# A fused attention and bilinear feed-forward kernel: the first batch's chain by token halves, the first up weights in 256 columns, the down weight in six transfers

## Chip, cores and metric

The kernel runs on one core of a Trainium2 chip (trn2). The metric is the device time of one execution in microseconds (us). The kernel before has a median of 243.78 us over five runs, from 243.56 to 244.42 us.

## What is computed

Eight batches of eight attention heads (576 tokens, head size 64) are reduced through 32 memory slots, and the result goes through a bilinear feed-forward layer. Cut to what matters:

```python
a   = softmax(phi, axis=2)                       # 8 x 8 x 576 x 32
k_m = einsum('bhsm,bhsd->bhmd', a, k)            # 32 keys per head
v_m = einsum('bhsm,bhsd->bhmd', a, v)            # 32 values per head
x   = softmax(q @ k_m.T / 8) @ v_m               # 4608 tokens x 512
out = ((x @ w_a) * (x @ w_b)) @ w_out            # 512 -> 1536 -> 512
```

Inputs and output are float32 in DRAM; inside, the kernel works in float16.

## The kernel before, in words

**Stages of one batch.** `exp_phi` (`exp0`, `exp1`) takes the exponentials of `phi` on ScalarE. `sums` (`ks0`, `ks1` for keys, `vs0`, `vs1` for values; 0 and 1 are the two groups of four heads) is 36 small products on TensorE that give the unnormalised means and their denominators. VectorE then takes a reciprocal (L265) and scales the mean (`kvm`, L266). `transpose` (`kt0`, `kt1`, `vt0`, `vt1`) turns the mean on TensorE, and VectorE copies the result out of PSUM into `kvT` (L277). `q_transpose` (`qt0` to `qt3`, L204) turns q on VectorE. `scores` (`s0`, `s1`) needs `kvT` and two of the four turned q pieces; `exp_scores` (`e0`, `e1`) is ScalarE. `denominators` (`den0`, `den1`) is a product with a matrix of ones for each half of the 576 tokens, followed by a logarithm on ScalarE (L316); `normalise` (`nr0`, `nr1`) is an exponential on ScalarE (L324) and a product on VectorE (L326) that gives the attention weights `A`.

**Fold and up.** The output of attention is never formed. `fold` (`v0a`: columns 0 to 511 of w_a; `v1b`: columns 512 to 1023 of w_b; the names with h, such as `hv0a`, take 256 columns) multiplies the means of the values into the up weights, and `take_fold` (`x0a` and so on) copies the two PSUM banks out as `vab`, one on ScalarE and one on VectorE. `up_half` then multiplies `vab` with `A` for 128 of the 1536 columns and one half of the tokens (288): `a3` is column block 3 of the w_a side for both halves, `a3.0` its first half, `b3` the w_b side. ScalarE copies the a side out (L601), VectorE multiplies it with the b side into `ht` (L604). One 256-column load therefore serves blocks 0 and 1, a 512-column load blocks 0 to 3.

**Down.** The first four blocks of 128 tokens are multiplied with `w_out` directly (`early_downs`, L390): 4 blocks by 12 products of 512 columns. They are handed out one product at a time wherever a plan says `y3` (three products). The order runs over parts of `w_out`: every block gets its products with part 0 before any gets part 1. All later blocks go in pairs through seven sums instead of eight (`two_downs`, L465), planned by a class `Work` that spreads products over the slots of a stage.

**What sets the order.** The schedule is written by hand. `chain(0, ...)` and `chain(1, ...)` are strings of the unit names above in the order of issue; each engine runs its own instructions in this order. `f8` in a string is eight products of zeros (`fill`, L151), which nothing reads. From batch 1 on, `ups` runs the up blocks and hangs other units on the slots between them. PSUM has eight banks, which `Banks` hands out in turn.

**Loads.** The first batch's k comes by two transfers on the queues of SyncE and ScalarE. All other loads are issued by GpSimd (POOL) in one queue, converting float32 to float16 on the way (phi stays float32). Their order before is: phi, q (two halves), v of batch 0; w_a and w_b columns 0 to 511; 512 to 1023; 1024 to 1535; the first third of w_out; phi, k and the first half of q of batch 1; the second third of w_out; the second half of q; v in two halves; the last third of w_out; and then batch 2 and batch 3. A load on this queue waits for the load eight places before it: the page of waits shows GpSimd's `phi` load waiting for `v` of batch 0, and each later one for the load eight places ahead. After them GpSimd computes `w_sums` (L432), sums of parts of w_out.

Of the kernel before, what the change touches and what calls it, by code (L numbers as in the profile page):

```python
# [8 lines left out]
F32 = mybir.dt.float32  # L9
F16 = mybir.dt.float16  # L10
AF = mybir.ActivationFunctionType
ALU = mybir.AluOpType

P = 128
CS = 16.0
# [3 lines left out]
def kernel(  # L19
# [11 lines left out]
    nc = tc.nc  # L31
# [44 lines left out]
    def load_phi(b):  # L76
        phis[b] = inp.tile([P, NHP, NI * M], F32, name="phi_sb")
        nc.gpsimd.dma_start(out=phis[b], in_=rows(phi, b))

    def load_k(b, hps=slice(0, NHP)):  # L80
        kvs[b] = kv_sbs[b % 2]
        nc.gpsimd.dma_start(out=kvs[b][:, 0, hps], in_=rows(k, b)[:, hps])

    def load_v(b, hps=slice(0, NHP)):
        nc.gpsimd.dma_start(out=kvs[b][:, 1, hps], in_=rows(v, b)[:, hps])

    def load_q(b, hps=slice(0, NHP)):
        if b not in qs:
            qs[b] = inp.tile([P, NHP, NI * D], F16, name="q_sb")
        nc.gpsimd.dma_start(out=qs[b][:, hps], in_=rows(q, b)[:, hps])  # L90
# [7 lines left out]
    def load_wab(lo, hi):  # L98
        nc.gpsimd.dma_start(out=wa_sb[:, :, lo:hi], in_=wa_rows[:, :, lo:hi])
        nc.gpsimd.dma_start(out=wb_sb[:, :, lo:hi], in_=wb_rows[:, :, lo:hi])  # L100

    def load_wo(n):
        sl = slice(4 * n, 4 * (n + 1))
        nc.gpsimd.dma_start(out=wo_sb[:, sl, :], in_=wo_rows[:, sl, :])


# [48 lines left out]
    nc.vector.memset(kv_sbs[0][:, 2], 1.0 / CS)  # L155
    for x in halves:
        nc.vector.tensor_copy(out=kvs[0][:, 0, x], in_=k_f32[:, x])
    load_wab(0, 512)

    ones = consts.tile([P, 4, 32], F16, name="ones")  # L160
    nc.vector.memset(ones, 1.0)
# [2 lines left out]
    nc.gpsimd.affine_select(out=ones, in_=ones, compare_op=ALU.is_ge, fill=0.0, base=31,  # L164
                            pattern=[[32, 4], [0, 32]], channel_multiplier=-1)
    load_wab(512, 1024)
    load_wab(1024, 1536)
    load_wo(0)
    load_phi(1)
    load_k(1)  # L170
    load_q(1, halves[0])
    load_wo(1)
    load_q(1, halves[1])
    for x in halves:
        load_v(1, x)
    load_wo(2)
    nc.gpsimd.memset(kv_sbs[1][:, 2], 1.0 / CS)

    attn = {}
    vabs = {}  # L180
# [6 lines left out]
    def units(b):  # L187
# [57 lines left out]
        def sums(g, x):  # L245

            if g == 0 and x == 0:
                t["kvm"] = mid.tile([P, 2, 2, D], F16, name="kvm")
                t["rphi"] = small.tile([P, 2], F32, name="rphi")
                t["kvT"] = mid.tile([P, 6, P], F16, name="kvT")  # L250
            part = (slice(0, 3, 2), slice(1, 2))[x]
            pk = banks.tile([P, 2 - x, D], F32, name="pk")
            for i in range(NI):
                for j in range(4):
                    r, hp = head(g, j)
                    nc.tensor.matmul(  # L256
                        pk[32 * j:32 * j + 32],
                        t["exp"][64 * r:64 * r + 64, hp, i, :],
                        kvs[b][64 * r:64 * r + 64, part, hp, D * i:D * (i + 1)],
                        start=(i == 0),  # L260
                        stop=(i == NI - 1),
                        tile_position=(64 * r, 32 * j),
                    )
            if x == 0:
                nc.vector.reciprocal(out=t["rphi"][:, g:g + 1], in_=pk[:, 1, 0:1])  # L265
            nc.vector.tensor_scalar(out=t["kvm"][:, g, x], in0=pk[:, 0], scalar1=t["rphi"][:, g:g + 1], scalar2=None,  # L266
                                    op0=ALU.mult)

        def transpose(g, x):
            pT = banks.tile([P, 2 - x, P], F16, name="pT")  # L270
            for y in range(2 - x):
                for z in range(4):
                    cols = (slice(y, D, 2), slice(32 * (z % 2), 32 * (z % 2) + 32))[x]
                    nc.tensor.transpose(out=pT[32 * z:32 * z + 32, y, :], in_=t["kvm"][:, g, x, cols],
                                        identity=ident, tile_position=(0, 32 * z))
            lo = 4 + g if x else 2 * g
            nc.vector.tensor_copy(out=t["kvT"][:, lo:lo + 2 - x], in_=pT)  # L277

        def scores(gs):
            if 0 in gs:  # L280
# [25 lines left out]
                nc.scalar.activation(out=Ev[:, g, :, z, :], in_=pss, func=AF.Exp, scale=1.0 / (8.0 * CS))  # L306
                banks.free(bank)

        def denominators(g):

            t["L", g] = small.tile([P, S], F32, name="L")
            for hf in range(2):
                sl = slice(HALF * hf, HALF * (hf + 1))
                pD = banks.tile([P, HALF], F32, name="pD")
                nc.tensor.matmul(pD, ones, t["E"][:, g, sl], start=True, stop=True)  # L315
                nc.scalar.activation(out=t["L", g][:, sl], in_=pD, func=AF.Ln)  # L316
# [36 lines left out]
        def one(f, *a):  # L353
            return lambda: f(*a)

        for z in range(2):
            u[f"exp{z}"] = one(exp_phi, z)
            u[f"ks{z}"] = one(sums, z, 0)
            u[f"kt{z}"] = one(transpose, z, 0)
            u[f"vs{z}"] = one(sums, z, 1)  # L360
            u[f"vt{z}"] = one(transpose, z, 1)
            u[f"s{z}"] = one(scores, (z,))
            u[f"e{z}"] = one(exp_scores, z)
            u[f"den{z}"] = one(denominators, z)
            u[f"nr{z}"] = one(normalise, z)
            for hf in range(2):
                u[f"nr{z}{hf}"] = one(normalise, z, slice(hf, hf + 1))
            for n in range(NCH):
                u[f"v{n}{'ab'[z]}"] = one(fold, 512 * n, 512 * (n + 1), (z,))
                u[f"x{n}{'ab'[z]}"] = one(take_fold, 512 * n, 512 * (n + 1), z)  # L370
            for n in range(2):
                u[f"hv{n}{'ab'[z]}"] = one(fold, 256 * n, 256 * (n + 1), (z,))
                u[f"hx{n}{'ab'[z]}"] = one(take_fold, 256 * n, 256 * (n + 1), z)
# [13 lines left out]
    def down_part(po, bank, cidx, lo, hi):  # L387
        pair, c = divmod(cidx, NI)
        for i in range(lo, hi):
            nc.tensor.matmul(po, ht[:, i, P * c:P * (c + 1)], wo_sb[:, i, :],  # L390
                             start=(i == 0), stop=(i == NFF - 1))
            if i == NFF - 1:
                banks.free(bank)
                o_sb = opool.tile([P, d_model], F32, name="o_sb")
                nc.scalar.mul(out=o_sb, in_=po, mul=1.0 / (CS * CS))
                for z in range(2):
                    slot = 2 * c + z
                    nc.sync.dma_start(out=out_rows[2 * pair + slot // NI, slot % NI],
                                      in_=o_sb[64 * z:64 * z + 64, :])
            yield  # L400
# [8 lines left out]
    def early_downs():  # L409

        pos = [banks.take([P, d_model], F32, "po", hold=True) for c in range(EARLY)]
        for n in range(3):
            for c in range(EARLY):
                yield from down_part(*pos[c], c, 4 * n, 4 * (n + 1))

# [248 lines left out]
    def chain(b, plan):  # L666


        for x in plan.split():
            if x[0] == "f":  # L670
                fill(int(x[1:]), 256)
            elif x[0] == "y":
                some(int(x[1:]))
            elif x[0] in "ab":
                i, _, hf = x[1:].partition(".")
                for h in ([int(hf)] if hf else (0, 1)):
                    up_half(b, int(i), h, "ab".index(x[0]))
            else:
                us[b][x]()

    fill(16)
    chain(0, "exp0 exp1 qt0 qt1 f12 ks0 f4 kt0 f2 ks1 f1 s0 e0 kt1 qt2 qt3 f2 den0 f4 s1 e1 nr0 f8 vs0 vs1 den1 f2 vt0 vt1 nr1 f4")
    chain(0, "v0a x0a f4 a0 a1 v0b x0b f4 b0 b1 a2 b2 v1a x1a a3 b3 a4 a5 v1b x1b a6 a7 b4 b5 v2a x2a b6 b7 a8 a9")
    load(2)
    chain(0, "v2b x2b a10 a11 b8 b9 b10 b11")
    chain(1, "exp0 y1 exp1 y11 ks0 ks1 y1 qt0 y3 kt0 qt1 s0 e0 kt1 y6 qt2 qt3 den0 y3 s1 nr0 y4 vs0 e1 vs1 den1 y1 vt1 y2 vt0 nr1 hv0a hx0a hv0b y2 hx0b y3")
    load(3)
    sum_weights()
    ups(steps(1, 0, 4), slots(1, "- hv1a+hx1a hv1b+hx1b+y1 - v1a+x1a y3+v1b x1b y3"))
    ups(half_steps(1, 0, 4), slots(1, "- v2a+x2a+v2b+x2b+qt0' - - qt1'+exp0'+qt2' exp1' - kv'+km'+y9"))  # L690
    work.plan(S + HALF, 10)
    ups(half_steps(1, 1, 4), slots(2, "qt3 kvt - sc+e0+e1 - den0+den1+nr0 - v0+nr1+x0a x0b - v1+x1b x1a"))
    second = "v2_+x2a_+exp0 x2b_ exp1 - kv+km qt0 kvt+qt1 - qt2+qt3 sc+e0 e1+v0+x0a den0+x0b nr0+v1+x1a L x1b+exp0' - exp1' v2+x2a den1+qt0' x2b - nr1+qt1'+kv'+km' - - qt2'+kvt'+qt3'"
    every = "- sc+e0 e1 den0 v0+x0a+x0b - - nr0+exp0' - - v1+x1a qt0' x1b+den1 exp1' - v2+x2a+x2b nr1+qt1' kv'+km' qt2' - qt3' - kvt'+L -"
    last = "sc+e0 - e1 - v0+x0b - x0a den1 - - den0 v1+x1b x1a+nr0 - - - - nr1+v2+x2a - - - - - x2b"
    for b in range(2, B):
# [37 lines left out]
```

## Time and profile before

| what | value |
|---|---|
| median of five runs | 243.78 us (243.56 to 244.42) |
| the profiled execution | 243.69 us |
| its span, first to last instruction | 242.0 us; 1.69 us lie around it |
| TensorE busy in the span | 233.0 us (96%) |
| VectorE, ScalarE, GpSimd busy | 167.2, 157.1, 155.9 us |
| mean granted TensorE clock | 0.999 |
| read from HBM, written | 42.47 MB, 9.44 MB |

Times inside the execution count from the start of the span. "L593" is line 593 of the kernel before. In the timeline view each row gives start, duration, engine, line, operation, output and inputs, how many instructions are merged, and in brackets how long the engine was idle before and what ended that. The chain of waits gives start, duration and the piece of work that carried the end. The tile view gives, for one load, when it was issued and how long after that it landed. The stretch of interest is the first 50 us; there the same loads, seen one by one in the tile view, land at these times (issue plus time to landing):

| load | issued | to landing | landed |
|---|---|---|---|
| q of batch 0, halves | 2.3, 3.0 | 6.7, 7.5 | 9.0, 10.5 |
| v of batch 0 | 3.7 | 9.6 | 13.3 |
| w_a, w_b columns 0 to 511 | 5.0, 5.8 | 11.7, 13.5 | 16.7, 19.3 |
| w_a, w_b columns 512 to 1023 | 8.3, 9.1 | 13.4, 15.3 | 21.7, 24.4 |
| w_a, w_b columns 1024 to 1535 | 9.8, 10.6 | 17.1, 19.0 | 26.9, 29.6 |
| w_out, first third | 11.3 | 20.7 | 32.0 |
| phi of batch 1 | 13.5 | 19.9 | 33.4 |
| k of batch 1 | 17.0 | 19.3 | 36.3 |
| q of batch 1, first half | 19.6 | 18.2 | 37.8 |
| w_out, second third | 22.1 | 18.2 | 40.3 |
| q of batch 1, second half | 24.7 | 17.0 | 41.7 |
| v of batch 1, halves | 27.2, 29.8 | 16.0, 14.8 | 43.2, 44.6 |
| w_out, last third | 32.3 | 14.8 | 47.1 |

### The profile page before, as it was taken

The numbers are of one execution on the slowest core, as the hardware profiler recorded it, in microseconds if no ns is written. First come the engines' busy times: TensorE is split into PE (matmuls) and PEld (weight loads), VectorE is DVE, ScalarE is ACT, GpSimd is POOL, SyncE is SP. The second block draws the span as 40 slices with busy tenths as digits, with TensorE's granted clock in tenths as the row PEclk, the third lists the DMA queues.
The fourth block names the chain that finished last, engine by engine and source line by source line (L and its number), as shares of the span: only waits on it lengthen the run. The fifth ranks groups of instructions, "written<-read, shape, count | busy, mean of one in ns | idle before, by whom it ended". The sixth has DMA issues, their size and how long they took to land.

```text
span 242.0 us, 7661 instructions
## 1 busy us (share of the span) xinstructions
PE 233.0 (96%) x3043; PEld 167.8 (69%) x3043; DVE 167.2 (69%) x402; ACT 157.1 (65%) x406; POOL 155.9 (64%) x130
## 2 busy tenths in 40 slices
PE   7889999999999999999999999999999999999993
PEld 2555664356757867777787777877787778888882
DVE  4536784478858868976984659875987586756652
ACT  2265771679597599598757777587856877465430
POOL 7822363499879549873989759882939087946001
PEclk9999999999999999999999999999999999999999
DMA  6999999999948948962279632795210303033154
GB/s 234 234 206 207 208 255 208 258 224 281 221 98 185 213 88 169 238 119 44 46 174 212 142 87 57 176 205 133 49 43 14 79 15 74 13 80 67 42 127 114
DMA packets 24659, 34.10 MB, mean 141 GB/s; under 512 B 1936, under 2 KB 18704, under 8 KB 24624
## 3 DMA queue, kind: packets, MB, share of 16 engines
q0 software_dynamic: 18160, 23.14, 51.1%
q1 hardware_dynamic: 5952, 9.70, 15.8%
q10 hardware_dynamic: 512, 0.79, 1.0%
q8 instruction: 23, 0.38, 0.6%
q14 instruction: 12, 0.10, 0.1%
HBM read 42.47 MB, written 9.44 MB: 214 GB/s over the span
## 4 chain that ended last, share of the span: by engine, by line
PE 88%; ACT 3%; DMA 3%; DVE 2%; issue 1%; POOL 0%; DVEq 0%; POOLq 0%
PE pa L593 20%; PE pb L593 19%; PE py L465 17%; PE pv L465 8%; PE pva L338 5%; PE po L390 5%; PE px L465 4%; DMA q_sb<-in_q_dram 3%; PE pkv L213 2%; PE pscore L293 2%; PE pD L315 2%; PE pk L256 1%; ACT E L306 1%; PE pT L242 1%; PE pw L151 1%
## 5 line engine op out<-in xcount | busy, mean ns | idle before, releaser
L604 DVE TENSOR_TENSOR ht<-a_sb,pb 128x288 f16<-128x288 f16 x168 | 73.2, 448 | 37.8 <-ACT a_sb L601 28.6
L593 PEld LDWEIGHTS <-vab 128*128 128x128 f16 x768 | 71.6, 98 | 27.1 <-issue 9.4
L601 ACT CAST a_sb<-pa 128x288 f16<-128x288 f32 x168 | 66.7, 408 | 26.0 <-PE pa L593 24.6
L593 PE MATMUL pa<-A,vab 128*128 128x288 f16 x384 | 75.9, 287 | 0.4 <-DVE vab L350 0.2
L593 PE MATMUL pb<-A,vab 128*128 128x288 f16 x384 | 75.1, 286 | 0.3 <-ACT vab L350 0.3
L447 POOL TENSOR_TENSOR h_sums<-ht 128x768 f16<-128x768 f16 x28 | 45.9, 1641 | 33.2 <-DVE ht L604 32.5
L465 PEld LDWEIGHTS <-h_sums 128*128 128x128 f16 x384 | 37.3, 98 | 7.0 <-issue 0.5
L350 DVE CAST vab<-pva 128x512 f16<-128x512 f32 (+1 forms) x50 | 32.3, 664 | 3.2 <-PE pva L338 2.6
L350 ACT CAST vab<-pva 128x512 f16<-128x512 f32 (+1 forms) x50 | 28.0, 584 | 8.6 <-PE pva L338 8.4
L465 PEld LDWEIGHTS <-ht 128*128 128x128 f16 x288 | 28.1, 98 | 5.6 <-issue 0.4
L465 PE MATMUL py<-w_sums,h_sums 128*128 128x256 f16 x192 | 30.4, 273 | 0.0
L447 POOL TENSOR_TENSOR h_sums<-ht,h_sums 128x768 f16<-128x768 f16 x14 | 23.0, 1641 | 1.0
L447 POOL TENSOR_TENSOR h_sums<-h_sums,ht 128x768 f16<-128x768 f16 x14 | 22.9, 1639 | 0.9
L306 ACT ACTIVATE E<-pscore 128x288 f16<-128x288 f32 x32 | 11.4, 418 | 13.6 <-PE pscore L293 13.6
L326 POOL TENSOR_TENSOR A<-E,R 128x576 f16<-128x576 f16 x12 | 15.3, 1277 | 7.4 <-ACT R L324 7.1
L465 PE MATMUL pv<-w_sums,h_sums 128*128 128x256 f16 x96 | 16.2, 273 | 0.0
L465 PE MATMUL py<-wo_sb,ht 128*128 128x256 f16 x96 | 16.0, 273 | 0.0
L472 ACT ACTIVATE u<-py 128x256 f32<-128x256 f32 x32 | 12.6, 392 | 5.0 <-PE py L465 4.8
L204 DVE STREAM_TRANSPOSE qT<-q_sb 128x288 f32<-128x288 f32 x32 | 14.4, 463 | 2.0 <-DMA q_sb<-in_q_dram 2.0
L465 PE MATMUL py<-w_sums,ht 128*128 128x256 f16 x96 | 15.5, 272 | 0.1
L465 PE MATMUL px<-wo_sb,ht 128*128 128x256 f16 x96 | 15.4, 273 | 0.0
L316 ACT ACTIVATE L<-pD 128x288 f32<-128x288 f32 x32 | 11.4, 424 | 4.7 <-PE pD L315 4.3
(65 smaller groups left out, 273.5 us busy)
## 6 DMA issues: line engine op xcount, KB each, us to landing
out_dram<-o_sb SPq DMA_DIRECT2D x68, 128.0 KB, 2.4
phi_sb<-in_phi_dram POOLq DMA_DIRECT2D x8, 576.0 KB, 6.0
kv_sb<-in_v_dram POOLq DMA_DIRECT2D x7, 576.0 KB, 10.7
kv_sb<-in_k_dram POOLq DMA_DIRECT2D x7, 576.0 KB, 7.5
q_sb<-in_q_dram POOLq DMA_DIRECT2D x6, 576.0 KB, 13.6
wa_sb<-in_moe_w_a_dram POOLq DMA_DIRECT2D x3, 512.0 KB, 13.4
wb_sb<-in_moe_w_b_dram POOLq DMA_DIRECT2D x3, 512.0 KB, 15.3
wo_sb<-in_moe_w_out_dram POOLq DMA_DIRECT2D x3, 512.0 KB, 18.2
```

What stands on the lines that cost most here:

```text
L204: nc.vector.transpose(out=t["qT"][:, hp, :].bitcast(F32), in_=qs[b][:, hp, :].bitcast(F32))
L306: nc.scalar.activation(out=Ev[:, g, :, z, :], in_=pss, func=AF.Exp, scale=1.0 / (8.0 * CS))
L326: engine.tensor_tensor(out=attn[b][:, g, sl], in0=t["E"][:, g, sl], in1=t["R", g][:, sl], op=ALU.mult)
L338: nc.tensor.matmul(t["pva", lo, z][g][0][32 * j:32 * j + 32, 0:hi - lo], t["kvT"][64 * r:64 * r + 64, 4 + g, M * j:M * j + M], w_sbs[z][64 ...
L350: engine_copy(out=vabs[b][z][:, g, lo:hi], in_=pva[:, 0:hi - lo])
L390: nc.tensor.matmul(po, ht[:, i, P * c:P * (c + 1)], wo_sb[:, i, :], start=(i == 0), stop=(i == NFF - 1))
L447: engine.tensor_tensor(out=out, in0=in0, in1=in1, op=op)
L465: nc.tensor.matmul(po, lhs[:, i], rhs[:, i], start=first and i == 0, stop=i == KH - 1, skip_group_check=not first)
L472: nc.scalar.mul(out=x, in_=po, mul=scale)
L593: nc.tensor.matmul(ps, vabs[b][x][:, g, P * i:P * (i + 1)], attn[b][:, g, HALF * hf:HALF * (hf + 1)], start=(g == 0), stop=(g == 1))
L601: nc.scalar.copy(out=a_sbs[b, i, hf], in_=ps)
L604: nc.vector.tensor_tensor(out=ht[:, i, t0:t0 + HALF], in0=a_sbs.pop((b, i, hf)), in1=ps, op=ALU.mult)
```

## The change

Five things are changed, all of them at the start of the program, except for one line of a later plan.

1. The first 512 columns of w_a and w_b come in four loads of 256 columns (a, b, a, b) where there were two. GpSimd's 2 us memset of batch 1's constant (L177 before) moves up between the loads of columns 512 and 1024.
2. w_out comes in six loads of two row blocks where there were three of four. The order is w_out 0 and 1, phi, k, first half of q, w_out 2 and 3, second half of q, v in two halves, w_out 4 and 5. `early_downs` runs over six parts accordingly.
3. The zero products are 128 columns wide (64 at the start and 18 more before the first sums; before, 16 of 512 and 12 of 256), and there are other numbers of them in the chain.
4. In batch 0, three of the four scalings of means (both k, and v of group 1) and the copies of their transposes go from VectorE to ScalarE.
5. The chain of batch 0 is written anew: both k sums run before the q transposes on VectorE's queue; denominators, normalisation and the first up blocks run by token halves; the first folds take 256 columns. The chain of batch 1 is reordered (the second k sum stands behind the first scores, and fewer early products stand ahead of the first), the slots of batch 1's ups move a few units, and one plan of batch 2 moves two units and a load.

```diff
     def load_wo(n):
-        sl = slice(4 * n, 4 * (n + 1))
+        sl = slice(2 * n, 2 * (n + 1))
...
-    load_wab(0, 512)
+    load_wab(0, 256)
+    load_wab(256, 512)
...
     load_wab(512, 1024)
+    nc.gpsimd.memset(kv_sbs[1][:, 2], 1.0 / CS)
     load_wab(1024, 1536)
-    load_wo(0)
-    load_phi(1)
-    load_k(1)
-    load_q(1, halves[0])
-    load_wo(1)
-    load_q(1, halves[1])
-    for x in halves:
-        load_v(1, x)
-    load_wo(2)
-    nc.gpsimd.memset(kv_sbs[1][:, 2], 1.0 / CS)
+    loads = {f"o{n}": lambda n=n: load_wo(n) for n in range(NFF // 2)}
...
+    for x in "o0 o1 p k q0 o2 o3 q1 v0 v1 o4 o5".split():
+        loads[x]()
...
-            nc.vector.tensor_scalar(out=t["kvm"][:, g, x], in0=pk[:, 0], scalar1=t["rphi"][:, g:g + 1], scalar2=None,
-                                    op0=ALU.mult)
+            if b == 0 and (x == 0 or g == 1):
+                nc.scalar.mul(out=t["kvm"][:, g, x], in_=pk[:, 0], mul=t["rphi"][:, g:g + 1])
+            else:
+                nc.vector.tensor_scalar(out=t["kvm"][:, g, x], in0=pk[:, 0], scalar1=t["rphi"][:, g:g + 1],
+                                        scalar2=None, op0=ALU.mult)
...
-            nc.vector.tensor_copy(out=t["kvT"][:, lo:lo + 2 - x], in_=pT)
+            engine_copy = nc.scalar.copy if b == 0 and (x == 0 or g == 1) else nc.vector.tensor_copy
+            engine_copy(out=t["kvT"][:, lo:lo + 2 - x], in_=pT)
...
-        for n in range(3):
+        for n in range(NFF // 2):
             for c in range(EARLY):
-                yield from down_part(*pos[c], c, 4 * n, 4 * (n + 1))
+                yield from down_part(*pos[c], c, 2 * n, 2 * (n + 1))
...
             if x[0] == "f":
-                fill(int(x[1:]), 256)
+                fill(int(x[1:]), P)
...
-    fill(16)
-    chain(0, "exp0 exp1 qt0 qt1 f12 ks0 f4 kt0 f2 ks1 f1 s0 e0 kt1 qt2 qt3 f2 den0 f4 s1 e1 nr0 f8 vs0 vs1 den1 f2 vt0 vt1 nr1 f4")
-    chain(0, "v0a x0a f4 a0 a1 v0b x0b f4 b0 b1 a2 b2 v1a x1a a3 b3 a4 a5 v1b x1b a6 a7 b4 b5 v2a x2a b6 b7 a8 a9")
-    load(2)
-    chain(0, "v2b x2b a10 a11 b8 b9 b10 b11")
-    chain(1, "exp0 y1 exp1 y11 ks0 ks1 y1 qt0 y3 kt0 qt1 s0 e0 kt1 y6 qt2 qt3 den0 y3 s1 nr0 y4 vs0 e1 vs1 den1 y1 vt1 y2 vt0 nr1 hv0a hx0a hv0b y2 hx0b y3")
+    fill(64, P)
+    chain(0, "exp0 exp1 f18 ks0 ks1 f4 kt0 qt0 qt1 f2 kt1 f4 qt2 qt3 f2 s0 e0 f2 den00 s1 e1 f8 den10 nr00 nr10 vs0 vs1 den01 den11 nr01 f4 vt0 vt1 hv0a nr11 hx0a f6 a0.0 a1.0 hv0b hx0b a0.1 a1.1 hv1a hx1a b0 b1 a3 hv1b a2 hx1b v1a x1a b2 b3 a4 a5 v1b x1b a6 a7 b4 b5 v2a x2a b6 b7 a8 a9 L v2b x2b a10 a11 b8 b9 b11 b10")
+    chain(1, "exp0 y3 exp1 y8 ks0 y1 qt0 y2 kt0 y2 qt1 s0 ks1 y3 e0 y1 kt1 qt2 y1 qt3 den0 y3 s1 y1 nr0 y4 vs0 e1 vs1 y1 den1 y2 vt0 vt1 nr1 y2 hv0a hx0a hv0b y1 hx0b y2")
     load(3)
     sum_weights()
-    ups(steps(1, 0, 4), slots(1, "- hv1a+hx1a hv1b+hx1b+y1 - v1a+x1a y3+v1b x1b y3"))
-    ups(half_steps(1, 0, 4), slots(1, "- v2a+x2a+v2b+x2b+qt0' - - qt1'+exp0'+qt2' exp1' - kv'+km'+y9"))
+    ups(steps(1, 0, 4), slots(1, "- y1+hv1a+hx1a hv1b+hx1b - y3+v1a+x1a y3+v1b+x1b - -"))
+    ups(half_steps(1, 0, 4), slots(1, "- v2a+x2a+v2b+x2b+qt0' - - qt1'+exp0' exp1'+qt2' - kv'+km'+y9"))
```

`den00` is `den0` for the first token half alone, and `nr10` is `nr1` for the first half.

## The prediction

> **What bounds the kernel now.** I read the page first, then busy time by microsecond, then the chain of waits, and last every load of the first 50 us in the tile view.
>
> ```profile
> PE 233.0 (96%) x3043; PEld 167.8 (69%) x3043; DVE 167.2 (69%) x402; ACT 157.1 (65%) x406; POOL 155.9 (64%) x130
> ...
> PE   7889999999999999999999999999999999999993
> ...
> DMA  6999999999948948962279632795210303033154
> ```
>
> TensorE is the bound: 233 of 242 us. What an edit at the start can win is time in which TensorE idles or multiplies zeros. The change touches neither the number nor the size of the useful products (two folds of 512 columns become four of 256). But the DMA row shows the other bound: its nines begin with the second slice (6 us) and run to about 66 us. So in this stretch each load lands when the bytes before it have passed, whatever the engines do. The chain of waits says where TensorE stands:
>
> ```profile
> 19.41 0.31 PE pa L593
> ...
> 21.59 1.16 PE pb L593 x8
> ...
> 31.15 0.34 PE pva L338 x8
> ...
> 34.54 2.59 PE po L390 x12
> 37.13 0.95 PE pk L256 x72
> ...
> 43.01 0.37 PE pscore L293 x16
> ```
>
> The first up products start at 19.41 us, the w_b ones only at 21.59. The last fold (v2b) is at 31.1, the end of batch 0's chain at 34.4, and batch 1's sums are at 37.1. From then on TensorE idles little: by the busy time per microsecond 0.43 us in 39 to 40, 0.05 in 40 to 41, 0.05 in 45 to 46, 0.33 in 46 to 47, and 0.4 us in all between 48 and 88. The timeline shows why I don't take this as room:
>
> ```profile
> 41.69 0.84 DVE L204 STREAM_TRANSPOSE qT<-q_sb 128x288 f32<-128x288 f32 x2 [0.62 <-DMA q_sb<-in_q_dram]
> ...
> 44.29 0.71 PEld L256 LDWEIGHTS <-exp_sb 64*32 64x32 f16 x72 [0.42 <-issue]
> ...
> 48.44 0.65 PE L593 MATMUL pa<-A,vab 128*128 128x288 f16 x4
> ```
>
> VectorE waited for q's second half and began the moment it landed (41.7). The values' sums run at 44.29; their second 36 products start near 44.65, and the data for these land at 29.8 + 14.8 = 44.6:
>
> ```profile
> L85 POOL DMA_DIRECT2D kv_sb<-in_v_dram x1: 696/696/696, 29.8 to 29.8; - x1
> ...
> DMA to landing us min/median/max: 14.8/14.8/14.8
> ```
>
> So batch 1 is already at the pace of its loads.
>
> **Step 1, landing times.** Total bytes are the same. The six up loads land 2.54 us apart (19.3 to 32.0 in five steps), 512 KB in 512 pieces of 1 KB: 79 ns for each of 32 pieces per DMA engine. k of batch 1 takes 2.9 us for 512 pieces of 1152 bytes: 90 ns. A line through both gives 10 ns for 128 bytes, so nearly all cost goes by bytes. The four 256-column loads have pieces of 512 bytes, which no row shows. From below: 0 (bytes alone). From above: such a piece costs what a 1 KB one does, and four loads take 4 x 2.54 where two did, +5.1 us. In between, at 0 to 9 ns fixed per piece (9 if I take 89 and 80 ns), 1024 more pieces over 16 engines cost 0 to 0.6. I take **0.3 us** for every later load: the two rows are the nearest. Five more issues on POOL cost 5 x 0.75 and the moved memset 2.04; POOL otherwise waits 1.8 us at nearly every load, with seven loads outstanding, so both are hidden. Landings then: 256-column loads 14.9, 16.5, 18.1, 19.6; next 22.0, 24.7, 27.2, 29.9; w_out 31.1, 32.3; phi 33.7; k 36.6; q 38.1; w_out 39.3, 40.6; q 42.0; v 43.5, 44.9; w_out 46.1, 47.4.
>
> The Trainium skill ("DMA: Bandwidth & Descriptors", section "Bandwidth") speaks against cutting loads: it gives a fixed 2.0 us per DMA and asks for 1 MiB or more. If the five additional loads each paid that in turn, I estimate 10 us more. Loads that queue here land 2.54 us apart for 512 KB and 1.45 us for 288 KB, in proportion to bytes, so the rows leave no room for that fixed part.
>
> **Step 2, batch 0's chain.** Zero products: a 512-column one takes 0.427 us at the start (the spacing of the weight loads until 5.5 us), so 128 columns take 0.107; later, six 128-column transposes take 0.34, or 0.057 each. About 40 slow and 42 fast ones end at 1.26 + 4.3 + 2.4 = 8.0, before phi's exponentials let the sums start (8.47, as now). From there: k sums to 9.75 (2 x 0.5); reciprocals no longer queue behind q's transposes (rphi at 9.25 rather than 9.76); a scaling on ScalarE lies between VectorE's 0.28 and ScalarE's 0.41 for 288 columns (below 0.28 is possible too); I take 0.3 as the tile has just 64 columns. kvT copies end at 10.7 and 11.1, the scores at 11.3, e0 at 12.1, s1 at 12.7, e1 at 13.5. v of batch 0 lands at 13.3; vs0, vs1 end at 14.8; logarithms and exponentials by halves (0.36 each on ScalarE) end at 16.3 and 16.6; kvT copy on VectorE, which now sits behind A's third half, at 16.8. hv0a 16.9, a0.0 17.7, hv0b 18.2, b0 19.2. That is **2.4 us earlier** than 21.59. The same products then stand ahead of v1a (a0 to a3, b0, b1: 2.2 us), so it could go at 21.4, but its weights come at 22.0; and v1b, v2a, v2b, which now run 1.5 to 1.9 us after their landings (23.66, 26.06, 28.47, 31.08), run at them. v2b to the end takes 3.29 us (31.08 to 34.37): 29.9 + 3.29 = **33.2**, a lead of 1.2 us. Cover: weights hide 0.6 us of any slip in this paragraph, and step 3 hides 1.0 more; if both are gone, each microsecond here is a microsecond of the total.
>
> The Trainium skill ("ScalarE: Activation LUTs", "Rules for kernel authors" and "What ACT_TABLE_LOAD costs") says to multiply on VectorE, and gives 186 ns + 0.833 ns per element, with 93 ns more for a scale from a pointer: an estimated 0.33 us per scaling. No run here shows one on ScalarE; three of them would add 0.15 us, within the cover.
>
> **Step 3, batch 1's chain.** Eleven products with w_out take 11 x 0.216 = 2.4, to 35.6. The k sums wait for k at 36.6: **1.0 us of the lead is gone**. First scores need two q transposes after 38.1, with a kvT copy (0.29) between them on VectorE: 38.1 + 0.47 + 0.29 + 0.47 = 39.4, while TensorE's work ahead (y1 y2 kt0 y2) ends at 38.5: another wait. s1 needs q's second half: 42.0 + 0.94 = 42.95, so it ends at 43.4, as before. Then y1, y4 and vs0 end at 44.8, and vs1 starts with v's second half at 44.9; before, 44.65. At this point both kernels have done the same work, 29 early products included: the lead is nil, or -0.25. What is left up to the first up product of batch 1 is vs1 0.45, den1 0.25, vt 0.37, folds 0.41, eight products 1.73: 3.2 us. Before, it took 3.8, since TensorE idled 0.38 for kvT. The path through ScalarE and VectorE (den1 at 45.5, logarithms, exponential, A, vab) opens a0 at 48.2. **48.25 against 48.44**: 0.2 us is left.
>
> **Step 4, the rest.** From 48 us on TensorE is full; the moved slots hold the same work. I cost them at 0, with 0.4 us of idle time up to 88 us as the most to be won, and as much to be lost.
>
> Sum: 243.69 (the profiled execution: span 242.0 and 1.69 around it) - 0.2 = **243.5 us**. The median of the five runs is 0.09 above that execution; I leave this aside.
>
> **Rivals.**
> - *The lead is kept.* If k, q and v of batch 1 don't hold TensorE, the 1.2 us of step 2 stay: 243.69 - 1.2 = 242.5, or 242.1 with the idle time of step 4. For it: only 0.62 us of waiting for a load shows there before. Against: the nines of the DMA row and the landing at 44.6.
> - *Small pieces are slow (slower).* In the 512-byte pieces of the first four loads: from 1.0 us of delay on, v's second half (45.6) puts a0 at 48.95, which is slower. At the bound of 5.1, vs1 waits until 49.7: +4.8, 248.5; half of it gives 246.0. Against: cost goes by bytes in the two rows.
> - *The chain of batch 0 comes late.* If the shorter zero products leave the clock low or ScalarE queues up, up to 1.6 us is covered; a slip of 2.6 costs 1.0, 244.7. All 82 zero products at 0.107 end at 10.0, 1.6 late, which is just covered.
> - *It does nothing:* the forecast comes close, as the loads decide.
>
> **How the numbers follow.** A measurement can tell 0.2% (0.49 us) from no change. Forecast 0.45 (own range 243.0 to 244.0: 0 to 0.6 of delay, 0.4 of step 4), lead kept 0.35, small pieces 0.10, late chain 0.10. Faster: 0.35 + 0.07 of the forecast = 0.42. Same: 0.38 + 0.02 of the late chain = 0.40. Slower: 0.18. Range 242.4 to 244.3; left out are the small pieces, part of the late chain and the far end of the kept lead.
>
> **What would show it.** In the profile after: w_b's second 256-column load landing near 19.6; b0 near 19.2; v2b near 29.9; first po near 33.2; a gap on TensorE before the k sums near 36.6; vs1 near 44.9; batch 1's first pa near 48.2. A po at 33.2 with vs1 well before 44.6 would show the kept lead; v2b after 31 would show slow pieces if the loads land late, a late chain if they don't.

## The result and the profile after

The changed kernel takes 243.79 us (median of 54 runs), the kernel before 243.93 us (94 runs). The ratio of their times is 0.9987, 95% interval 0.9979 to 0.9995: about 0.3 us faster, less than the 0.2% that one measurement can tell. The prediction was 243.5 us, range 242.4 to 244.3. Some runs of seven of these kernels take 258 to 261 us (7 of 94 before, 3 of 54 after; 3 of 12 in experiment 2, 4 of 12 in 4 and in 8, 1 of 6 in 7, 2 of 12 in 12), which the medians hold and the ratios leave out.

This is the page of the changed kernel's profiled run (244.64 us, span 242.9); the rows answer to those shown of before:

```profile
PE 233.2 (96%) x3110; PEld 171.2 (70%) x3110; DVE 165.9 (68%) x400; ACT 159.7 (66%) x416; POOL 159.3 (66%) x135
...
PE   7869999999999999999999999999999999999993
...
PEclk9976999999999999999999999999999999999999
DMA  6999999999946953993169642795220303032154
```

The PEclk row holds something new: 7 and 6 in the third and fourth slice. By stretches (busy us of PE, PEld, DVE, ACT, POOL, then the granted clock, the DMA share and GB/s):

```profile
13.00:15.00 2.00, 0.90 (x25) 0.51 (x9) 0.00 (x0) 1.00 (x3) 0.44 (x2) 1.00 1.45 194
...
16.00:18.00 2.00, 1.44 (x21) 0.79 (x14) 1.25 (x5) 2.00 (x7) 0.96 (x2) 0.50 1.45 197
...
20.00:22.00 2.00, 2.00 (x22) 0.81 (x22) 0.42 (x1) 1.64 (x5) 0.31 (x1) 0.50 1.24 205
```

In this run TensorE had half its clock from about 15.4 to 22.2 us. Of the other 51 runs, 22 have a mean clock below 0.99 (median 244.03) and 29 one of at least 0.996 (median 243.42). To compare stage with stage I use a run at full clock: experiment 1, the same kernel again (243.49 us, span 241.8). In its timeline the start of the first up product with w_b, the last fold, the first early product, the first k sums and the first up product of batch 1 stand here:

```profile
14.54 0.28 PE L151 MATMUL pw<-warm 128*128 128x128 f16 x2 [1.16 <-issue]
...
17.73 0.30 PE L342 MATMUL pva<-wa_sb,kvT 64*32 64x256 f16 x8 [0.78 <-DVE kvT L280]
...
20.18 0.30 PE L598 MATMUL pb<-A,vab 128*128 128x288 f16 x1
20.75 1.03 PE L598 MATMUL pb<-A,vab 128*128 128x288 f16 x7 [0.27 <-issue]
...
23.92 1.15 PE L598 MATMUL pb<-A,vab 128*128 128x288 f16 x8 [0.48 <-ACT vab L354]
...
31.00 0.41 PE L342 MATMUL pva<-wb_sb,kvT 64*32 64x512 f16 x8
34.29 1.89 PE L395 MATMUL po<-wo_sb,ht 128*128 128x512 f16 x8
...
36.77 0.69 PE L255 MATMUL pk<-kv_sb,exp_sb 64*32 64x128 f16 x36
...
48.15 0.65 PE L598 MATMUL pa<-A,vab 128*128 128x288 f16 x4
```

The w_b products start 1.4 us earlier than before (21.59), but the first early product only 0.08 (before: 34.37 in the same view, in the row below), and batch 1's first up product 0.29 (48.44):

```profile
34.37 2.75 PE L390 MATMUL po<-wo_sb,ht 128*128 128x512 f16 x12
```

The loads land thus (predicted in brackets): 256-column loads 15.6 (14.9), 17.1 (16.5), 18.3 (18.1), 19.6 (19.6); then 22.2 (22.0), 24.8 (24.7), 27.3 (27.2), 29.8 (29.9); k 36.6 (36.6), q 38.1 (38.1) and 42.1 (42.0).

Cut into stages, the profiled runs say where the time went. Starts of instructions, in us; the last column ends at the start of the last products:

| profiled run | first early product | from there to batch 1's first up product | to batch 2's sums | to the last products |
|---|---|---|---|---|
| before | 34.37 | 14.07 | 11.99 | 176.54 |
| after, full clock (exp. 1) | 34.29 | 13.86 | 12.30 | 176.33 |
| difference | -0.08 | -0.21 | +0.31 | -0.21 |

The sum is -0.19, the difference of the spans 242.0 and 241.8. The third stage repeats well: 11.99 us in the three profiles of the old start with the old slots of batch 1 (before, experiments 10 and 11), 12.30 in eight with the new. The last stage took 176.54 with the old plan of batch 2 (before, experiment 10), and with the new one 176.31 to 176.35 in seven profiles, but 176.48 and 176.61 in two.

### The profile page after: what moved, and what is told of

The parts are those of the page before. It is cut to its first block, busy times and chain, and to the rows that moved or that the text cites. A ratio compares the mean times of both kernels' runs of the same rounds, so it can differ in the third digit from the quotient of the medians.

```text
span 242.9 us, 7804 instructions
## 1 busy us (share of the span) xinstructions
PE 233.2 (96%) x3110; PEld 171.2 (70%) x3110; DVE 165.9 (68%) x400; ACT 159.7 (66%) x416; POOL 159.3 (66%) x135
## 4 chain that ended last, share of the span: by engine, by line
PE 90%; DMA 3%; ACT 2%; DVE 2%; issue 2%; DVEq 0%; POOLq 0%
PE pa L598 21%; PE pb L598 19%; PE py L470 17%; PE pv L470 9%; PE pva L342 6%; PE po L395 5%; PE px L470 4%; DMA phi_sb<-in_phi_dram 3%; PE pkv L212 2%; PE pscore L296 2%; PE pD L319 2%; PE pk L255 1%; PE pw L151 1%; PE pT L241 1%; DVE ht L609 1%
## 5 line engine op out<-in xcount | busy, mean ns | idle before, releaser
L606 ACT CAST a_sb<-pa 128x288 f16<-128x288 f32 x168 | 66.9, 407 | 26.2 <-PE pa L598 24.7
L598 PE MATMUL pa<-A,vab 128*128 128x288 f16 x384 | 76.9, 290 | 0.1
L470 PE MATMUL px<-wo_sb,ht 128*128 128x256 f16 x96 | 15.4, 273 | 0.0
L194 ACT ACTIVATE exp_sb<-phi_sb 128x576 f16<-128x576 f32 x16 | 11.0, 705 | 5.4 <-DMA phi_sb<-in_phi_dram 5.4
```

What stands on the lines that cost most here:

```text
L470: nc.tensor.matmul(po, lhs[:, i], rhs[:, i], start=first and i == 0, stop=i == KH - 1, skip_group_check=not first)
L598: nc.tensor.matmul(ps, vabs[b][x][:, g, P * i:P * (i + 1)], attn[b][:, g, HALF * hf:HALF * (hf + 1)], start=(g == 0), stop=(g == 1))
L606: nc.scalar.copy(out=a_sbs[b, i, hf], in_=ps)
```

## Experiments

Each run stands beside the kernel before on the same chip (median 243.81 us in experiments 1 to 4, 243.94 in 5 to 8, 244.05 in 9 to 12).

**1. The changed kernel again.**

> The changed kernel once more, nothing edited, to see a second profile. Its first profile has a granted TensorE clock of 0.5 from 15.7 to 22.1 us and a mean of 0.986, and of its runs those with a mean clock of 0.99 or more have a median of 243.42 us, the others 244.04. Loads theory (the prediction's): in a profile with the full clock the first early product stands near 33.2 us (before: 34.4), and the lead is gone at batch 1's first up product (48.0 to 48.4, before 48.44). Rival, lead kept: 47.2 or earlier there. If the profile has the low clock again, the first early product is after 35.

243.41 us, ratio 0.9976 (0.9957 to 0.9996). Stages as above: batch 1's first up product (48.15) stands where the loads theory had it, the first early product (34.29) does not.

**2. The start's zero products as before.**

```diff
-    fill(64, P)
+    fill(16)
+    fill(12, 256)
```

and no `f18` ahead of the sums.

> The changed kernel with the start's zero products as before (16 of 512 columns and 12 of 256, so 28 instead of 82). Both profiles show TensorE waiting for nothing that the profile names after exactly 223 matmuls: before 0.64 us at 15.60, after 1.10 us at 13.70. Theory A (the stall belongs to a place in TensorE's instruction stream): it moves 54 matmuls later, to the second scores or the values' sums, and ends at about the same time (14.8), so the wait is shorter, TensorE's busy share from 12 to 15 us rises and the clock falls in fewer runs than 22 of 51: median 243.4 to 243.6. Theory B (the stall is a wait for data at that point of the chain): it stays ahead of the first den of group 1, 1.1 us, and the clock falls as often: median 243.8.

243.52 us, ratio 0.9978 (0.9957 to 0.9999). v of batch 0 lands at 13.6, not 14.5, and the first early product starts at 33.63, 0.74 ahead of before. TensorE's stall moved behind 51 of the 72 value products, as theory A had it. This is part of the lead that the prediction spoke of, and the timelines of TensorE and then of VectorE show where it goes:

```profile
33.63 2.54 PE L395 MATMUL po<-wo_sb,ht 128*128 128x512 f16 x11
36.44 0.68 PE L255 MATMUL pk<-kv_sb,exp_sb 64*32 64x128 f16 x36 [0.28 <-DMA kv_sb<-in_k_dram]
...
42.89 0.80 PE L296 MATMUL pscore<-qT,kvT 32*32 32x288 f16 x16 [0.54 <-DVE qT L203]
...
48.27 0.65 PE L598 MATMUL pa<-A,vab 128*128 128x288 f16 x4
```

```profile
42.36 0.84 DVE L203 STREAM_TRANSPOSE qT<-q_sb 128x288 f32<-128x288 f32 x2 [0.88 <-DMA q_sb<-in_q_dram]
```

TensorE waits 0.28 us for k, then 0.54 for the turned q, whose second half lands at 42.3. Batch 1's first up product is at 48.27, no earlier than the 48.15 of experiment 1. An earlier batch 0 is given back at batch 1's loads.

**3. The later zero products 256 columns wide.**

```diff
-                fill(int(x[1:]), P)
+                fill(int(x[1:]), P if x == "f18" else 256)
```

> The changed kernel with the 32 later zero products of batch 0's chain 256 columns wide instead of 128, the same number (the 82 at the start stay). If the short zero products let the clock fall, TensorE is busier by up to 32 x 0.055 = 1.8 us between 9.9 and 19 us, the clock holds in more runs than 29 of 51, and the median is 243.4 to 243.6. If the fall comes from the 1.1 us stall alone, the clock falls as often and the median stays at 243.8; wide products on the path then cost at most 0.3 us more at the first up product, which the loads hide.

243.39 us, ratio 0.9967 (0.9945 to 0.9988): as experiment 1. None of its 12 runs lost clock (mean 0.996 or more in all); of experiment 1's 12, two did. That fits a clock that falls with sparse work, but with so few runs it is not shown; and in its profile the stall was 0.23 us where experiment 1 had 1.16, so wide products and a short stall are not told apart.

**4. The first up weights in 512-column loads again.**

```diff
-    load_wab(0, 256)
-    load_wab(256, 512)
+    load_wab(0, 512)
```

> The changed kernel with the first up weights in two loads of 512 columns again (two loads fewer; the rest as changed). Loads theory: the w_b side comes at 19.3 us and not at 16.7, so the first w_b block stands near 20.6 instead of 19.2 and the lead at the first early product falls from 1.2 to at most 0.8 us; at batch 1's first up product nothing is left of either, so the time is that of the changed kernel within 0.2 us (at equal clock). Rival, lead kept: slower than the changed kernel by 0.5 us or more.

243.23 us, ratio 0.996 (0.9935 to 0.9985), the best so far. By the windows, first of experiment 1, then of this one:

```profile
13.00:16.00 3.00, 1.84 (x86) 1.41 (x85) 0.24 (x1) 1.71 (x7) 1.07 (x3) 1.00 1.44 195
```

```profile
13.00:16.00 3.00, 2.07 (x87) 1.46 (x85) 0.47 (x2) 1.96 (x8) 1.64 (x3) 1.00 1.25 206
```

The 512-byte pieces keep the DMA engines busier (1.44 against 1.25) at 195 instead of 206 GB/s. Without them k of batch 1 lands at 36.1 instead of 36.6, and everything from the first early product (33.88) to the end comes 0.4 us sooner. At full clock the medians are 243.03 and 243.40: 0.37 us faster, where the loads theory had allowed 0.2 and its rival had expected a loss. The lead at the first early product rose to 0.49 us instead of falling.

**5 and 6. The loads relieved: before and after without a third of the up weights.** The products of that third read columns 512 to 1023 again, so the output is not that of the layer.

```diff
-    load_wab(1024, 1536)
...
-                            w_sbs[z][64 * r:64 * r + 64, hp, lo:hi],
+                            w_sbs[z][64 * r:64 * r + 64, hp, min(lo, 512):min(hi, 1024)],
```

> The kernel before, but columns 1024 to 1535 of w_a and w_b are never loaded (that third of the up work reads columns 512 to 1023 again), so 1 MB of loads is left out and everything behind it lands some 5.1 us earlier: w_out near 26.9, k near 31.2, q near 32.7 and 36.6, v near 38.1 and 39.5. Pace theory (mine: from the first up products on, batch 1 goes at the pace of its loads): the waits for q (0.62 on VectorE) and for v at 44.6 go, the first pa of batch 1 comes 0.5 to 0.8 earlier than 48.44, and the median is 0.5 to 0.8 below that of the kernel before. Work theory (rival: TensorE's own work sets batch 1, the loads land just in time by accident): pa stays within 0.2 of 48.44, the median within 0.3.

> The changed kernel with the same load left out. Pace theory as the prediction had it: with batch 1's loads out of the way the lead of batch 0's chain is kept, the first pa of batch 1 at about 47.2 and the median 1.0 below 243.4. Work theory: the first run's profile shows no lead at the first po (34.29 against 34.37) and nearly no wait for k or v, so the relief changes little: po stays near 34.3, pa near 48.2, and the median is 0 to 0.3 below 243.4. The kernel before gains more from the relief than the changed one by work theory, less by pace theory.

258.07 and 257.05 us: 13 us slower, which no theory of mine had. VectorE's and GpSimd's timelines of experiment 6 say why:

```profile
46.61 12.97 DVE L329 TENSOR_TENSOR A<-E,R 128x576 f16<-128x576 f16 x1 [0.36 <-ACT R L327]
```

```profile
46.50 3.24 POOL L436 TENSOR_TENSOR w_sums<-wo_sb 128x768 f16<-128x768 f16 x2
...
56.05 3.21 POOL L436 TENSOR_TENSOR w_sums<-wo_sb,w_sums 128x768 f16<-128x768 f16 x2
```

VectorE's product for batch 1's second A, 0.46 us before, took 12.97. It began 0.1 us after GpSimd's first `w_sums` and ended at 59.58, 0.3 us after the eighth. With earlier loads `w_sums` had come ahead of A; in the changed kernel they start 0.9 us after A's end (48.78 and 47.85). Up to that point experiment 6 answers the question it was made for: from the first early product (34.03) to batch 1's first up product (47.37) it needs 13.34 us, not 13.86.

**7. Batch 1's order as before, in the changed kernel** (the string of `chain(1, ...)`, the two `ups` lines of batch 1 and the line `second`).

> The changed kernel with the order of batch 1's chain, the slots of batch 1's ups and the one plan of batch 2 put back as before. If what is won lies in batch 1's new order (step 3 has 0.55 us there, 3.2 instead of 3.8 us from the values' second sum to the first pa): pa near 48.7, median 243.8 to 243.9, as before. If it lies in batch 0's chain or in the loads: pa within 0.15 of 48.3 and the median stays at 243.4.

245.98 us, ratio 1.0071 (1.0046 to 1.0095). The second stage takes 14.32 us, as expected 0.5 more than 13.86. But the third takes 13.37 us, where the kernel before needs 11.99 with the same strings, and the last 176.93. So the old order of batch 1 costs more after the new start than it did after the old one, and the parts of the change can't be added up one by one. Why is open: whether the six transfers of w_out or the banks of PSUM that the new start leaves behind do this was not tried.

**8. Experiments 2 and 4 together.**

> The changed kernel with the first up weights in 512-column loads again and the start's zero products as before (16 of 512 columns and 12 of 256; no 18 before the sums). With 512-column loads alone v of batch 0 landed at 14.2 instead of 13.3, with the wide start alone at 13.6, and TensorE's stall fell behind the 223rd matmul in each run. If TensorE's instructions come in by transfers that pass through the same DMA engines, and come later when fewer matmuls stand ahead: v lands at 13.3 to 13.5, the stall lies in the values' sums behind 51 of 72 products, and batch 0's chain gets up to 0.7 us earlier: first po 33.5 or later, median 242.9 to 243.2. If v's landing has another reason it stays at 14.2, and the median at that of the 512-column loads alone, 243.2 to 243.3. By the pace theory k and v of batch 1 (36.2 and 44.4) hold pa at 47.8 either way.

243.45 us, ratio 0.9966 (0.9948 to 0.9984). v of batch 0 lands at 13.2 (13.3 to 13.5 expected) and the stall lies behind 51 of 72 value products, as expected. No time is won over experiment 4: the stall (0.78 us) now falls into the sums themselves, and the first early product is at 33.84 (33.88 there).

**9 and 10. The relieved loads without the collision.** As 6 and 5, with

```diff
+    held = consts.tile([P, 1], F16, name="held")
+    nc.gpsimd.tensor_copy(out=held, in_=attn[1][:, 1, 0:1])
     sum_weights()
```

> The changed kernel without the loads of columns 1024 to 1535 of w_a and w_b (as in the run before of that kind), and with one 128x1 copy on GpSimd, ahead of w_sums, that reads batch 1's second A; so w_sums can't start before that product of VectorE has ended. Collision theory (the 13 us came from VectorE's A and GpSimd's w_sums at the same time): A takes 0.46 us again, not 12.97, and the 13 us are gone. Pace theory: without waits for q and v the first pa of batch 1 comes near 47.5 instead of 48.31 (the run before had its A 0.78 us earlier), and the median is 242.6 to 242.9. Work theory: pa stays near 48.2, median 243.3. If the 13 us have another cause (the repeated columns, say), they stay.

> The kernel before with the same two edits. Collision theory: no 13 us. Pace theory: the 0.62 us wait for q goes and pa comes 0.4 to 0.7 before 48.44; median 243.2 to 243.4. If batch 0's chain of the changed kernel has any lead at all that the loads take back, the changed kernel gains more from the relief than this one; if it has none, both gain the same, 0.4 to 0.8.

243.20 us, ratio 0.9981 (0.9956 to 1.0007), and 243.99 us, ratio 0.9994 (0.9977 to 1.0011). The 13 us are gone; VectorE's product in experiment 9:

```profile
47.39 0.46 DVE L329 TENSOR_TENSOR A<-E,R 128x576 f16<-128x576 f16 x1 [0.36 <-ACT R L327]
```

Four of experiment 9's runs lost clock; its eight others have a median of 242.93, against 243.40 for those of experiment 1 in another session: 0.47 us. The ratios to the kernel before (0.9981 here, 0.9976 in experiment 1) don't show this gain; the stage does: it takes 13.33 us instead of 13.86. Batch 1's first up product stands at 48.14 and not near 47.5, because this profile reached the first early product only at 34.81. The kernel before wins nothing from the same relief. In experiment 10 its second stage is 14.06 (14.07 before), and TensorE has the same waits, for VectorE's `kvT` and not for a load. First before, then experiment 10:

```profile
39.67 0.82 PE L293 MATMUL pscore<-qT,kvT 32*32 32x288 f16 x16 [0.40 <-DVE kvT L277]
...
47.01 0.30 PE L338 MATMUL pva<-wa_sb,kvT 64*32 64x256 f16 x8 [0.33 <-DVE kvT L277]
```

```profile
40.26 0.82 PE L292 MATMUL pscore<-qT,kvT 32*32 32x288 f16 x16 [0.40 <-DVE kvT L276]
...
47.59 0.30 PE L337 MATMUL pva<-wa_sb,kvT 64*32 64x256 f16 x8 [0.33 <-DVE kvT L276]
```

All of experiment 10 stands some 0.6 us later; its granted clock was 0.50 from about 11.2 to 14.6 us.

**11. The kernel before with the plan of batch 2 alone** (the line `second`: L behind `exp0'`, `x0b` and `qt1'` a slot earlier, `kv'+km'` behind `qt2'`).

> The kernel before with one line of the change: the plan of batch 2 that moves two units and a load. In the profiles the changed kernel is 0.13 us ahead at batch 1's first pa, nothing ahead at the batch 2 sums at 60.4 and at the batch 3 sums at 97.1, and 0.16 to 0.19 ahead from batch 3's scores at 102.0 on, which took 0.56 before and 0.40 after. If that line is all that is won: the scores at 102 take 0.40, the end comes 0.16 earlier, median 243.6, at the same bounds as the changed kernel. If the gain comes from the start: no difference from the kernel before.

243.79 us, ratio 0.9999 (0.9975 to 1.0023): nothing that the times can tell. The timelines tell it, first before, then experiment 11; what counts is from the start of the scores to the next row:

```profile
102.02 0.63 PE L293 MATMUL pscore<-qT,kvT 32*32 32x288 f16 x32
102.58 0.42 PE L593 MATMUL pa<-A,vab 128*128 128x288 f16 x2
```

```profile
102.76 0.47 PE L293 MATMUL pscore<-qT,kvT 32*32 32x288 f16 x32
103.17 0.42 PE L593 MATMUL pa<-A,vab 128*128 128x288 f16 x2
```

0.56 became 0.41, and the last stage 176.31 instead of 176.54. The profiled run as a whole is later because the stall of TensorE in its values' sums was 1.54 us, not 0.64.

**12. A version meant to beat both: 512-column loads, and q's second half ahead of w_out's fourth transfer.**

```diff
-    for x in "o0 o1 p k q0 o2 o3 q1 v0 v1 o4 o5".split():
+    for x in "o0 o1 p k q0 o2 q1 o3 v0 v1 o4 o5".split():
```

> A version meant to beat both: the changed kernel with the first up weights in 512-column loads again, and the fourth transfer of w_out moved behind q's second half (order o2, q1, o3 instead of o2, o3, q1). The scores of batch 1's second group took 0.73 us with q's second half landing in their midst, and 0.38 without that wait. Pace theory: q's second half lands near 40.4 instead of 41.6, these scores take 0.38, batch 1's first pa comes at 47.4 to 47.7 instead of 47.88 (v's second half, landing at 44.4, takes back part), and the median is 242.9 to 243.1 against 243.23. Work theory: no change from 243.2.

243.71 us, ratio 0.998 (0.9959 to 1.0001); of its ten runs below 245 us five lost clock, and the other five have a median of 243.03, that of experiment 4. Nothing is won. In the profiled run the second group's scores no longer wait for q, but that run lost clock and was late, so it can't show whether v took the gain back. Experiment 4 stays the best version that was run, by its median.

## Why the prediction came out right, step by step

The total was right: 243.5 predicted, 243.4 at full clock, 243.79 over all runs. That it was right is in part luck. Of its four steps the landing times held, batch 0's chain failed, batch 1's chain ended where it was to end with half of its reason wrong, and the rest came to 0 by two terms that cancel.

**Step 1, landing times: right.** I took 0.3 us of delay for later loads. Experiment 4 alone puts it at 0.5 for k (36.1 against 36.6). Over the profiles of the new order with all loads, k lands at 36.1 to 36.3 with 512-column loads (experiments 4, 8, 12) and at 36.3 to 36.6 with 256 columns (the profile of the result, experiments 1, 2, 3, 7): 0.3 in the mean. The bytes decided, not the number of loads: the 256-column loads land 1.3 to 1.4 us apart. The fixed 2 us for each DMA ("DMA: Bandwidth & Descriptors", section "Anatomy of one DMA — SWDGE (gpsimd) path", of the Trainium skill) don't appear between these landings. v of batch 0 was missed: predicted 13.3, landed 14.5.

**Step 2, batch 0's chain: failed.** "29.9 + 3.29 = 33.2, a lead of 1.2 us" became 34.29, a lead of 0.08. The w_b products were to start at 19.2 and started at 20.18: v of batch 0 landed 1.2 us late, and TensorE stood still for 1.16 us ahead of the value sums. Experiments 2, 4 and 8 separate the causes of v's delay: 512-column loads and the old start give 13.2, the short zero products alone 14.2, the small pieces alone 13.6, both 14.5. But in experiment 2 q, which was asked for ahead of any piece, landed 0.46 late already (10.82 against 10.36 in 8). Counted from q's second half, v comes 2.8 us later in all six profiles with the old start, with either size of pieces, and 3.7 to 4.1 in all eight with the new one. So the start's 82 short zero products in place of 28 cost v 0.9 to 1.3 us, and no cost of the pieces to v shows. From the w_b products to the first early product before needed 12.78 us and the changed kernel 14.11. Of these 1.33 us, 0.48 are a wait for ScalarE's copy of the fold, 0.27 another stall, and 0.23 the `hv1b` that stood ahead of this point before; 0.35 are spread thin. The cover of 0.6 us that the weights were to give was used up: the first 512-column fold ran at 23.03 and the last at 31.00, 0.8 and 1.2 us after their weights had landed (22.2 and 29.8), so by then TensorE's own work, not the loads, paced batch 0. The ScalarE scalings were sized well: 0.31 us each, I had 0.3.

**Step 3, batch 1's chain: the end right, the reason half.** "48.25 against 48.44" was measured as 48.15. The claim that a lead of batch 0 is lost at k and q is shown by experiment 2 (0.28 and 0.54 us of waits, a lead of 0.74 gone). But in the changed kernel there was no lead to lose, and the reading that the kernel before "is already at the pace of its loads" is wrong: relieved of 1 MB it wins nothing (experiment 10). It was held by its own order, with two waits for VectorE. The new order needs 13.33 us for this stage where the old needs 14.07; the loads leave 0.21 of these 0.74, which is why the sum came out. Two profiles with all loads show the 13.33 too, that of the result and that of experiment 12: they reached the first early product only at 35.71 and 35.08, so that the loads were there in time. The last part of step 3 was right: 3.2 us from the values' second sum to the first up product, measured 3.14 (45.01 to 48.15). That VectorE began the moment q's half landed was true and decided nothing, since TensorE's work ahead of those scores ended no earlier. The chain of waits of experiment 1 shows that it does decide now:

```profile
30.11 11.95 DMA q_sb<-in_q_dram
42.06 0.02 issue
42.08 0.85 DVE qT L203 x2
42.93 0.04 issue
42.97 0.44 PE pscore L296 x14
```

**Step 4, the rest: 0 in sum, by two terms that cancel.** With the new slots of batch 1 the stage from batch 1's first up product to batch 2's sums is 0.31 us longer in every profile; that the slots alone do it is not shown, since with the old ones behind the new start it takes 13.37 us (experiment 7). The new plan of batch 2 wins about 0.2, of which 0.15 at batch 3's scores (experiment 11). I had bounded both at 0.4 without telling them apart.

**The rivals.** *The lead is kept* is out: what lead there is goes at the loads. *Small pieces are slow* stayed far below its point of 1.0 us of delay. *The chain of batch 0 comes late* came true in part: in 22 of 51 runs the clock fell, and those are 0.6 us longer; in the profiled one the first early product came at 35.71 and batch 1's first up product at 49.04. That short zero products are the reason was not settled. *It does nothing* lies close: the interval 0.9979 to 0.9995 leaves out 1, but 0.3 us is less than the 0.49 that one measurement can tell.

**What the times hold beyond the profiles.** In the first four experiments' session the kernel before ranged from 243.50 to 244.43 us between its quartiles, experiment 1 from 243.38 to 243.49; their fastest runs, 243.26 and 243.19, hardly differ. The profiled runs of the kernel before and its variants had stalls of 0.64 us (243.69 us), 1.54 us (experiment 11, 244.56 us), 1.77 us (experiment 5) and none (experiment 10, with 3.4 us at half clock), those with the new start 0.91 to 1.16 where the zero products were 128 wide throughout. A good part of what the median gained may thus be a start that varies less, but few starts were profiled, and this is argued, not shown.

## What to carry to other kernels

A wait that ends when a load lands doesn't show that loads set the pace: take some bytes away and see whether the end moves. An earlier first stage is worth only what the next stage's loads leave of it, so cost the two as a race and not as a sum. And before a transfer is made earlier, look at what it releases on the other engines: here 1 MB less to load made a kernel 13 us slower.

## What the runs showed of the hardware

- **TensorE stalled after 223 matmuls.** In every profile but experiment 10's, which shows none, a stall with no releaser ("issue") stands after exactly 223 matmuls, whatever they are: in the values' sums before, between zero products after, and after 51 value products when the start had 28 zero products. In experiments 1, 6, 7 and 9 a second one follows 128 matmuls later. The row of experiment 2:

```profile
15.33 0.34 PE L255 MATMUL pk<-kv_sb,exp_sb 64*32 64x64 f16 x21 [0.49 <-issue]
```

  The page lists a queue for instructions, here of experiment 1:

```profile
q8 instruction: 24, 0.39, 0.7%
```

  24 packets of 0.39 MB are about 16 KB each. 3110 matmuls with as many weight loads make 6220 instructions, so I estimate that a packet holds some 256 of them, or 128 matmuls with their loads, the distance of the two stalls; with 3043 matmuls before there are 23 packets (but 24 in experiment 5, with as many matmuls). I take the stall for a wait on the next packet of TensorE's instructions, behind the loads in the same DMA engines, and v's late landing with 54 more zero products for the other side of it. The position is shown; that cause fits and was not tested further. If it holds, zero products are not free: they use up instructions.

- **VectorE was shut out for as long as GpSimd had work.** One VectorE product of two f16 tensors in SBUF took 12.97 us through eight GpSimd operations of some 1.6 us (experiment 6; 13.02 in 5) and took 0.46 when GpSimd was held back (9 and 10). The Trainium skill ("SBUF — State Buffer", section "SBUF: two separate sides") has an exclusive lock on a port that VectorE and GpSimd share, held for one whole instruction. The runs agree on the lock but not on its length: by that rule VectorE would have got its turn after the one operation that was running.

- **The clock can fall without a long gap.** In the changed kernel's profiled run the granted clock went to 0.50 at about 15.4 us although no gap between TensorE's products ahead of it was over 1.1 us; in the two us from 13 to 15 it was busy for 0.90. The Trainium skill ("TensorE: Matmul & The Clock Gate", section "HAM oscillation — how this bites in real kernels") warns of gaps above 3.4 us; here the clock fell with none so long, in 22 of 51 runs of one kernel. The profiles show what goes with it. A fall lasts 3.41 us or a multiple (3.41 in experiment 10, 6.83 after and in 12, 13.65 in 6). I divided all 14 profiles into steps of 3.41 us from the clock's first rise, which comes at 4.3 to 6.7 us, differently in each run. Where the clock is full and TensorE is busy for at most 1.92 us of a step, the next step has a clock of 0.50 (six steps: 0 to 1.92 us); from 1.96 us on it stays full (all others). The closest two, experiment 12, where it fell, and 11, where it held:

```profile
11.15:14.56 3.41, 1.92 (x44) 0.83 (x33) 0.18 (x1) 1.80 (x5) 2.96 (x5) 1.00 1.23 208
```

```profile
13.56:16.97 3.41, 1.96 (x77) 1.32 (x77) 0.65 (x2) 1.56 (x4) 0.65 (x1) 1.00 1.24 207
```

  By these figures, whether a run of the same kernel loses clock depends on how its stall and its gaps fall into the steps.
